# Holding k's scaling and the pooled q, k and v of a pair of heads behind the softmax of the pair one back

## The chip, the cores and the metric

One core of a Trainium2 chip runs the whole program. The metric is the device time of one execution in microseconds (us). The engines are TensorE (PE, with its weight loads as PEld), VectorE (DVE), ScalarE (ACT), GpSimd (POOL) and the DMA queue of SyncE (SPq).

## What is computed

q, k and v have 2 batches of 8 heads, 576 positions and 64 columns. Each head's attention is the sum of two: a local one, in which a position sees those fewer than 4 away, and a pooled one on the means of 4 neighbouring positions, whose result is repeated 4 times. The result x (1152 tokens of 512) goes through a gated layer and then through 8 experts that share the tokens:

```python
q_d = q.reshape(B, H, Sd, factor, D).mean(axis=3)   # k_d and v_d alike
out_up = np.repeat(sm_attn(q_d, k_d, v_d), factor, axis=2)
mask = np.abs(pos[:, None] - pos[None, :]) < factor
scores = np.where(mask, scale * np.matmul(q, k.transpose(0, 1, 3, 2)), -1000000000.0)
...
x = (silu(x @ w_gate) * (x @ w_val)) @ w_out
...
out += P[:, e:e + 1] * (np.maximum(x @ w1[e], 0.0) @ w2[e])
```

## The kernel before

**Attention.** Heads are worked in 8 pairs (pr 0 to 7; a head h is one of 0 to 15). For a pair, `pooled` scales k on ACT (L368) and makes the pooled k and q by sums of 4 on DVE (kd L369, qd L376), with a small scaling of kd on ACT (L370). `scores` of a head writes a mask and the products of five windows of 128 into PSUM (tiles s, L390 to L397) and the pooled products (L399). DVE takes the row minima (stm, L402 to L404), ACT seven exponentials per head (ex, L408 to L413) that also add up the rows, DVE adds and inverts the sums (rs, L416 and L417), and POOL multiplies ex by them (L419, L421). `turn` transposes ex on PE (t, L430 to L435) and ACT copies it out (at, L436 to L438). `combine` multiplies a pair's two heads by v and by the pooled v (o, L450 and L457); DVE adds both parts up as x (L466), and `split` cuts x into two f16 halves, xhl, the high one on ACT (L166) and the low one on DVE (L167). `pooled_v` makes the pooled v (vdz) by three additions on POOL (L381 to L383). `x1_scale` finds a scale for all of a batch's x by products of v on PE (vv, L341), whose maximum DVE reads (mxv, L344).

**Beside it** the weights of the gated layer are prepared. `conv_gv` turns one of 12 blocks of 64-bit numbers (rawg, 1 MB each) into f32: one operation on ACT (L198, or L195 from the sixth block on), four on DVE (cvg, L199 to L202), and a largest value on ACT (L217). `prep_gv` splits the block into two f16 halves (gv, L166 and L167). `gv_step(c, f)` is 24 or 48 products by block f for the tokens of chunk c, and a few operations on ACT and DVE behind them (act, L543 to L560). Chunk 0 holds the first 512 tokens, which pairs 0 to 3 complete; chunk 1 needs all pairs. So gv(0,0) to gv(0,3) can run on PE while batch 1 is still in attention, and gv(1,0) ends the dependence on it. The rest (output layer, routing, experts) follows, most of it products on PE.

**What sets the order.** `attention` is a generator that is advanced step by step; scores run four heads ahead of the transposes (AHEAD). A list scheduler gives each engine a fixed order of instructions, in which it works strictly one after the other: an instruction that waits holds back all behind it. A block under `gate(x)` puts its instructions of x's engine behind x in that order; it adds no semaphore. Buffers also bind: k and q have 3 slots, v4 has 4, the PSUM tiles s, t and o share 6 banks (two per tile), rawg and cvg have 2 buffers each.

Of the kernel before, what the change touches and what calls it, by code (L numbers as in the profile page):

```python
# [11 lines left out]
AF = mybir.ActivationFunctionType  # L12
ALU = mybir.AluOpType
AX = mybir.AxisListType
# [4 lines left out]
FAC, SD = 4, 144  # L19
# [5 lines left out]
HS = SD // 2  # L25
# [13 lines left out]
DO = NW * P  # L39
# [21 lines left out]
def tile_kernel(ctx, tc, qT, kT, vw, vd4, wgv, wo, wg2, w1, w2, out):  # L61
    nc = tc.nc
    V, A, G, T = nc.vector, nc.scalar, nc.gpsimd, nc.tensor
# [143 lines left out]
    def gate(after):  # L207
        return tc.issue_after(after.ins) if after else nullcontext()
# [148 lines left out]
    def attention():  # L357
# [2 lines left out]
            return [psa.tile([P, 512], F32, tag="att", bufs=6, name=f"{nm}_{i}") for i in range(2)]  # L360

        qd, kd, exs, ats = {}, {}, {}, {}

        def pooled(pr):
            q, k = qz[pr % NQ], ld[pr]
            qd[pr] = ap.tile([P, 2, SD], F32, tag="qd", name=f"qd{pr}")
            kd[pr] = ap.tile([P, SD], F32, tag="kd", name=f"kd{pr}")
            A.activation(k, k, AF.Copy, scale=-0.125)  # L368
            V.tensor_reduce(kd[pr], k.rearrange("p (s a) -> p s a", a=FAC), axis=AX.X, op=ALU.add)  # L369
            A.activation(kd[pr], kd[pr], AF.Copy, scale=1.0 / (FAC * FAC))  # L370
            if pr not in QDV:
                t = ap.tile([P, 2, 2 * SD], F32, tag="qt", bufs=1, name=f"qt{pr}")
                G.tensor_tensor(t, q[:, :, 0::2], q[:, :, 1::2], op=ALU.add)
                G.tensor_tensor(qd[pr], t[:, :, 0::2], t[:, :, 1::2], op=ALU.add)
            else:
                V.tensor_reduce(qd[pr], q.rearrange("p j (s a) -> p j s a", a=FAC), axis=AX.X, op=ALU.add)  # L376

        def pooled_v(pr):
            v4, vd = v4s[pr], vdz[pr % 2]
            vt = ap.tile([HS, 2, 2, P], F32, tag="vt", bufs=1, name=f"vt{pr}")  # L380
            G.tensor_tensor(vt[:, 0], v4[:, :, 0], v4[:, :, 1], op=ALU.add)  # L381
            G.tensor_tensor(vt[:, 1], v4[:, :, 2], v4[:, :, 3], op=ALU.add)
            G.tensor_tensor(vd, vt[:, 0], vt[:, 1], op=ALU.add)  # L383

        def scores(h):
            pr, j = h // 2, h % 2
            q, k = qz[pr % NQ], ld[pr]
            nm = f"{h}"
            ps = bank(f"s{nm}")
            T.matmul(ps[0], lhsT=identb, rhs=maskb.rearrange("p u w -> p (u w)"), start=True, stop=False)  # L390
            for w in range(NW - 1):
                ws = slice(WSTART[w], WSTART[w] + P)
                T.matmul(ps[0][:, w * P:(w + 1) * P], lhsT=q[:, j, ws], rhs=k[:, ws],
                         start=False, stop=w == NW - 2)
            T.matmul(ps[1][:, DW:DW + P], lhsT=identb, rhs=maskb[:, 0], start=True, stop=False)
            ws = slice(WSTART[4], WSTART[4] + P)
            T.matmul(ps[1][:, DW:DW + P], lhsT=q[:, j, ws], rhs=k[:, ws], start=False, stop=True)  # L397
            for t in range(2):
                T.matmul(ps[1][:HS, t * SD:(t + 1) * SD], lhsT=qd[pr][:, j, t * HS:(t + 1) * HS],  # L399
                         rhs=kd[pr], start=True, stop=True)  # L400
            mx, sm = stm[h % 2], sts[h % 2]
            V.tensor_reduce(mx[:, :4], ps[0].rearrange("p (u w) -> p u w", u=4), axis=AX.X, op=ALU.min)  # L402
            V.tensor_reduce(mx[:, 4:5], ps[1][:, DW:DW + P], axis=AX.X, op=ALU.min)
            V.tensor_reduce(mx[:HS, 5:7], ps[1][:HS, :DW].rearrange("p (u w) -> p u w", u=2),  # L404
                            axis=AX.X, op=ALU.min)
            ex = ap.tile([P, NW * P + DW], F32, tag="ex", bufs=6, name=f"ex{nm}")
            for w in range(4):
                A.activation(ex[:, w * P:(w + 1) * P], ps[0][:, w * P:(w + 1) * P], AF.Exp, scale=-1.0,  # L408
                             bias=mx[:, w:w + 1], accum_out=sm[:, w, 0:1])
            A.activation(ex[:, DO - P:DO], ps[1][:, DW:DW + P], AF.Exp, scale=-1.0,  # L410
                         bias=mx[:, 4:5], accum_out=sm[:, 4, 0:1])
            for t in range(2):
                A.activation(ex[:HS, DO + t * SD:DO + (t + 1) * SD], ps[1][:HS, t * SD:(t + 1) * SD], AF.Exp,  # L413
                             scale=-1.0, bias=mx[:HS, 5 + t:6 + t], accum_out=sm[:HS, 5 + t, 0:1])
            rs = ap.tile([P, 8], F32, tag="rs", name=f"rs{nm}")
            V.tensor_reduce(rs, sm, axis=AX.X, op=ALU.add)  # L416
            V.reciprocal(rs, rs)  # L417
            x = ex[:, :DO].rearrange("p (w k) -> p w k", w=NW)
            G.tensor_tensor(x, x, rs[:, :NW, None].to_broadcast([P, NW, P]), op=ALU.mult)  # L419
            x = ex[:HS, DO:].rearrange("p (t k) -> p t k", t=2)  # L420
            G.tensor_tensor(x, x, rs[:HS, 5:7, None].to_broadcast([HS, 2, SD]), op=ALU.mult)  # L421
            exs[h] = ex

        def turn(h):
# [430 lines left out]
```

## Time and profile before

| | us |
|---|---|
| median of 3 runs (lowest, highest) | 1033.76 (1032.47, 1036.16) |
| profiled execution, first to last instruction | 1030.5 |
| median less that span (what lies around it) | 3.3 |
| PE busy, share of the span | 1002.1, 97% |
| DVE busy | 757.6, 74% |
| ACT busy | 456.2, 44% |
| POOL busy | 77.7, 8% |

The page gives no time of its own for the profiled execution, so the span is set against the median of the runs. Busy shares are means over stages: attention takes the first tenth of the span, and there DVE, ACT and POOL work hardest; afterwards PE runs almost without a pause. Times of rows count from the span's start.

### The profile page before, as it was taken

To read this page: it belongs to the slowest core of one execution; us is meant where nothing else is said; L and a number is where in the kernel's file an instruction comes from. 1 tells how busy PE (TensorE), PEld (TensorE's weight loads), DVE (VectorE), ACT (ScalarE), POOL (GpSimd) and SP (SyncE) were. 2 spreads that over 40 slices of the span, in tenths; PEclk is the share of its full clock that TensorE was granted. 3 is DMA by queue.
4 is the path that set the end of the run, shared out by engine and by line. 5 is a ranking of instruction groups with operands and counts; after the bars stand their busy time and mean duration, and the time that the engine had idled before them with its cause. 6 is when DMAs were issued, how large, how long until landed. Compare 5 with 4: busy or idle time off the path is not lost.

```text
span 1030.5 us, 16425 instructions
## 1 busy us (share of the span) xinstructions
PE 1002.1 (97%) x6545; PEld 637.1 (62%) x6545; DVE 757.6 (74%) x1556; ACT 456.2 (44%) x957; POOL 77.7 (8%) x100
## 2 busy tenths in 40 slices
PE   5889999999999999999999999999999999999998
PEld 4776555665568657556565756656665575565644
DVE  5799688885765998697488759749766984974721
ACT  6899547675443745254145215323512521541300
POOL 5575000000000200000000000000000000000000
PEclk9999999999999999999999999999999999999999
DMA  9632224230020013103012112101301211020011
GB/s 222 194 102 73 111 89 164 109 137 1 1 83 1 17 66 123 42 5 118 1 42 83 41 41 79 45 3 40 123 1 42 82 42 41 1 83 1 1 41 52
DMA packets 13115, 65.54 MB, mean 64 GB/s; under 512 B 1712, under 2 KB 1968, under 8 KB 6640
## 3 DMA queue, kind: packets, MB, share of 16 engines
q1 hardware_dynamic: 13040, 64.51, 17.8%
q8 instruction: 51, 0.84, 0.3%
q14 instruction: 24, 0.20, 0.1%
HBM read 62.14 MB, written 2.36 MB: 63 GB/s over the span
## 4 chain that ended last, share of the span: by engine, by line
PE 82%; DVE 9%; DMA 4%; ACT 3%; issue 2%; SPq 0%; ACTq 0%; DVEq 0%
PE y L174 36%; PE p L174 31%; PE gv L174 9%; PE wo L174 4%; DMA vz<-in_vw 1%; DMA rawg<-in_wgv 1%; DMA rawo<-in_wo 1%; DMA k<-in_kT 1%; DVE cvg L201 1%; DVE w L167 1%; DVE xhl L167 1%; PE lgps L585 1%; DVE cvg L202 1%; ACT ex L408 0%; DMA qz<-in_qT 0%
## 5 line engine op out<-in xcount | busy, mean ns | idle before, releaser
L174 PE MATMUL y<-w,hhl 128*128 128x512 f16 (+1 forms) x1752 | 396.2, 376 | 0.0
L174 PE MATMUL p<-bop,w 128*128 128x320 f16 (+1 forms) x2688 | 354.4, 286 | 0.8 <-DVE u L727 0.5
L174 PEld LDWEIGHTS <-w 128*128 128x128 f16 x2688 | 263.0, 98 | 90.6 <-issue 1.3
L174 PEld LDWEIGHTS <-hhl 128*128 128x128 f16 x1752 | 171.5, 98 | 178.2
L755 ACT ACTIVATE hhl<-h 128x640 f16<-128x640 f32 (+1 forms) x128 | 83.2, 676 | 160.9 <-DVE h L727 160.9
L174 PE MATMUL gv<-xhl,gv 128*128 128x320 f16 (+1 forms) x864 | 142.3, 326 | 3.4 <-ACT act L556 1.4
L166 ACT ACTIVATE w<-r,s_w 128x256 f16<-128x256 f32 (+1 forms) x96 | 71.2, 783 | 117.3 <-PE y L174 86.3
L786 DVE SCALAR_TENSOR_TENSOR acc<-y,pe,acc 128x512 f32<-128x512 f32 (+1 forms) x64 | 47.3, 738 | 101.3 <-PE y L174 100.5
L174 PEld LDWEIGHTS <-gv 128*128 128x128 f16 x864 | 84.2, 98 | 59.5 <-issue 5.5
L756 DVE SCALAR_TENSOR_TENSOR hhl<-h,hhl 128x640 f16<-128x640 f32 (+1 forms) x128 | 94.3, 753 | 15.5 <-ACT hhl L755 14.2
L727 DVE SCALAR_TENSOR_TENSOR h<-p,u 128x256 f32<-128x256 f32 (+1 forms) x192 | 84.9, 452 | 19.3 <-PE p L174 13.5
L167 DVE SCALAR_TENSOR_TENSOR w<-r,s_w,w 128x256 f16<-128x256 f32 (+1 forms) x96 | 78.0, 832 | 16.7 <-ACT w L166 16.7
L174 PE MATMUL wo<-ahl,wo 128*128 128x320 f16 (+1 forms) x432 | 71.5, 326 | 0.0
L166 ACT ACTIVATE w<-cmb,s_w 128x512 f16<-128x512 f32 x64 | 43.0, 710 | 42.1 <-DVE cmb L271 39.9
L727 DVE SCALAR_TENSOR_TENSOR u<-p,u 128x320 f32<-128x320 f32 (+1 forms) x128 | 57.3, 448 | 4.1 <-PE p L174 3.2
L174 PEld LDWEIGHTS <-wo 128*128 128x128 f16 x432 | 42.3, 99 | 26.9
L153 POOL PARTITION_ALL_REDUCE g_w<-gm_w x16 | 6.3, 394 | 592.7 <-DVE gm_w L149 586.7
L744 ACT ACTIVATE s<-p 128x256 f32<-128x256 f32 (+1 forms) x64 | 25.4, 397 | 55.8 <-PE p L174 55.7
L143 DVE TENSOR_REDUCE mxw<-r 128x1 f32<-128x1024 f32 x32 | 37.4, 1213 | 12.8 <-DMA r<-in_w 12.8
L167 DVE SCALAR_TENSOR_TENSOR w<-cmb,s_w,w 128x512 f16<-128x512 f32 x64 | 46.0, 740 | 0.1
L291 ACT ACTIVATE j<-r 128x1024 f16<-128x1024 f32 x32 | 33.4, 1046 | 25.4 <-DMA r<-in_w 25.4
L167 DVE SCALAR_TENSOR_TENSOR ahl<-act,sc,ahl 128x512 f16<-128x512 f32 (+1 forms) x24 | 19.6, 818 | 17.1 <-ACT ahl L166 17.1
(199 smaller groups left out, 914.8 us busy)
## 6 DMA issues: line engine op xcount, KB each, us to landing
r<-in_w SPq DMA_DIRECT2D x32, 1024.0 KB, 4.8
rawg<-in_wgv SPq DMA_DIRECT2D x12, 1024.0 KB, 4.8
rawo<-in_wo SPq DMA_DIRECT2D x6, 1024.0 KB, 6.8
vz<-in_vw SPq DMA_DIRECT2D x8, 320.0 KB, 5.9
k<-in_kT SPq DMA_DIRECT2D x8, 288.0 KB, 3.5
qz<-in_qT SPq DMA_DIRECT2D x16, 144.0 KB, 5.0
v<-in_vd SPq DMA_DIRECT2D x8, 288.0 KB
out<-acc SPq DMA_DIRECT2D x8, 256.0 KB, 2.0
```

The source lines that it names most:

```text
L143: V.tensor_reduce(o, i, axis=axis, op=ALU.max, apply_absolute_value=True)
L166: return (A.activation(hi, src, AF.Copy, scale=s), V.scalar_tensor_tensor(lo, src, s, hi, op0=ALU.mult, op1=ALU.subtract))
L167: V.scalar_tensor_tensor(lo, src, s, hi, op0=ALU.mult, op1=ALU.subtract))
L174: T.matmul(ps, lhsT=wf(i, k), rhs=xf(j, k), start=n == 0, stop=n == 3 * nk - 1)
L201: V.scalar_tensor_tensor(o, hi, 0xC0000000, o, op0=ALU.bitwise_and, op1=ALU.bitwise_or)
L202: V.scalar_tensor_tensor(o, lo, 29, o, op0=ALU.logical_shift_right, op1=ALU.bitwise_or)
L291: A.activation(junk, t[:, 2 * j:2 * j + 2].rearrange("p a n -> p (a n)"), AF.Abs, accum_out=mx[:, 2 * i + j:2 * i + j + 1])
L727: V.scalar_tensor_tensor(o, ps, HSC, u, op0=ALU.mult, op1=ALU.add)
L744: A.activation(s1, p1, AF.Copy, scale=HSC)
L755: ra = A.activation(t[:, 0], h, AF.Relu)
L756: rv = V.scalar_tensor_tensor(t[:, 1], h, 0.0, t[:, 0], op0=ALU.max, op1=ALU.subtract)
L786: V.scalar_tensor_tensor(acc[t][:, ds], ps, p[:, t:t + 1], acc[t][:, ds], op0=ALU.mult, op1=ALU.add)
```

## The change

Three dictionaries keep, for each head, its last exponential on ACT (`exped`), its reciprocal on DVE (`summed`) and its last multiplication on POOL (`scaled`). From the third pair on, k's scaling is put behind the last exponential of the pair one back, and the pooled k and q behind its reciprocal. The pooled v of the second to eighth pair is put behind the last multiplication of the pair one back. No instruction is added or taken away.

```diff
--- before.py
+++ after.py
@@ -360,27 +360,32 @@
             return [psa.tile([P, 512], F32, tag="att", bufs=6, name=f"{nm}_{i}") for i in range(2)]
 
         qd, kd, exs, ats = {}, {}, {}, {}
+        exped, summed, scaled = {}, {}, {}
 
         def pooled(pr):
             q, k = qz[pr % NQ], ld[pr]
             qd[pr] = ap.tile([P, 2, SD], F32, tag="qd", name=f"qd{pr}")
             kd[pr] = ap.tile([P, SD], F32, tag="kd", name=f"kd{pr}")
-            A.activation(k, k, AF.Copy, scale=-0.125)
-            V.tensor_reduce(kd[pr], k.rearrange("p (s a) -> p s a", a=FAC), axis=AX.X, op=ALU.add)
+            with gate(exped.get(2 * pr - 1) if pr > 1 else None):
+                A.activation(k, k, AF.Copy, scale=-0.125)
+            with gate(summed.get(2 * pr - 1) if pr > 1 else None):
+                V.tensor_reduce(kd[pr], k.rearrange("p (s a) -> p s a", a=FAC), axis=AX.X, op=ALU.add)
             A.activation(kd[pr], kd[pr], AF.Copy, scale=1.0 / (FAC * FAC))
             if pr not in QDV:
                 t = ap.tile([P, 2, 2 * SD], F32, tag="qt", bufs=1, name=f"qt{pr}")
                 G.tensor_tensor(t, q[:, :, 0::2], q[:, :, 1::2], op=ALU.add)
                 G.tensor_tensor(qd[pr], t[:, :, 0::2], t[:, :, 1::2], op=ALU.add)
             else:
-                V.tensor_reduce(qd[pr], q.rearrange("p j (s a) -> p j s a", a=FAC), axis=AX.X, op=ALU.add)
+                with gate(summed.get(2 * pr - 1) if pr > 1 else None):
+                    V.tensor_reduce(qd[pr], q.rearrange("p j (s a) -> p j s a", a=FAC), axis=AX.X, op=ALU.add)
 
         def pooled_v(pr):
             v4, vd = v4s[pr], vdz[pr % 2]
             vt = ap.tile([HS, 2, 2, P], F32, tag="vt", bufs=1, name=f"vt{pr}")
-            G.tensor_tensor(vt[:, 0], v4[:, :, 0], v4[:, :, 1], op=ALU.add)
-            G.tensor_tensor(vt[:, 1], v4[:, :, 2], v4[:, :, 3], op=ALU.add)
-            G.tensor_tensor(vd, vt[:, 0], vt[:, 1], op=ALU.add)
+            with gate(scaled.get(2 * pr - 1)):
+                G.tensor_tensor(vt[:, 0], v4[:, :, 0], v4[:, :, 1], op=ALU.add)
+                G.tensor_tensor(vt[:, 1], v4[:, :, 2], v4[:, :, 3], op=ALU.add)
+                G.tensor_tensor(vd, vt[:, 0], vt[:, 1], op=ALU.add)
 
         def scores(h):
             pr, j = h // 2, h % 2
@@ -410,15 +415,16 @@
             A.activation(ex[:, DO - P:DO], ps[1][:, DW:DW + P], AF.Exp, scale=-1.0,
                          bias=mx[:, 4:5], accum_out=sm[:, 4, 0:1])
             for t in range(2):
-                A.activation(ex[:HS, DO + t * SD:DO + (t + 1) * SD], ps[1][:HS, t * SD:(t + 1) * SD], AF.Exp,
-                             scale=-1.0, bias=mx[:HS, 5 + t:6 + t], accum_out=sm[:HS, 5 + t, 0:1])
+                e = A.activation(ex[:HS, DO + t * SD:DO + (t + 1) * SD], ps[1][:HS, t * SD:(t + 1) * SD], AF.Exp,
+                                 scale=-1.0, bias=mx[:HS, 5 + t:6 + t], accum_out=sm[:HS, 5 + t, 0:1])
+            exped[h] = e
             rs = ap.tile([P, 8], F32, tag="rs", name=f"rs{nm}")
             V.tensor_reduce(rs, sm, axis=AX.X, op=ALU.add)
-            V.reciprocal(rs, rs)
+            summed[h] = V.reciprocal(rs, rs)
             x = ex[:, :DO].rearrange("p (w k) -> p w k", w=NW)
             G.tensor_tensor(x, x, rs[:, :NW, None].to_broadcast([P, NW, P]), op=ALU.mult)
             x = ex[:HS, DO:].rearrange("p (t k) -> p t k", t=2)
-            G.tensor_tensor(x, x, rs[:HS, 5:7, None].to_broadcast([HS, 2, SD]), op=ALU.mult)
+            scaled[h] = G.tensor_tensor(x, x, rs[:HS, 5:7, None].to_broadcast([HS, 2, SD]), op=ALU.mult)
             exs[h] = ex
 
         def turn(h):
```

What it does to the engines' orders is shown at three places. Numbers in names are those of heads (ex, s, at, t, stm), pairs (k, kd, qd, x, o) or weight blocks (rawg, cvg, gv); the last number of a name is the buffer's. Lines of the changed kernel stand five or six further down.

ACT at the start, from the exponentials of head 2 to the first transposed copy. Before:

```order
L370 ACTIVATE kd2_321<-kd2_321 128x144
L368 ACTIVATE k3_217<-k3_217 128x576
L408 ACTIVATE ex2_251,sts0_114<-s2_0_237,stm0_112 128x128 x4
L410 ACTIVATE ex2_251,sts0_114<-s2_1_238,stm0_112 128x128
L413 ACTIVATE ex2_251,sts0_114<-s2_1_238,stm0_112 72x144 x2
L368 ACTIVATE k4_291<-k4_291 128x576
L408 ACTIVATE ex3_278,sts1_115<-s3_0_264,stm1_113 128x128 x4
L410 ACTIVATE ex3_278,sts1_115<-s3_1_265,stm1_113 128x128
L413 ACTIVATE ex3_278,sts1_115<-s3_1_265,stm1_113 72x144 x2
L370 ACTIVATE kd3_506<-kd3_506 128x144
L198 ACTIVATE cvg0_312<-rawg0_310 128x1024
L436 COPY at0_297<-t0_0_295 128x512
```

With the change, from the exponentials of head 3 to those of head 4:

```order
L413 ACTIVATE ex3_278,sts1_115<-s3_0_264,stm1_113 128x128 x4
L415 ACTIVATE ex3_278,sts1_115<-s3_1_265,stm1_113 128x128
L418 ACTIVATE ex3_278,sts1_115<-s3_1_265,stm1_113 72x144 x2
L442 COPY at0_297<-t0_0_295 128x512
L443 COPY at0_297<-t0_1_296 128x128
L444 COPY at0_297<-t0_1_296 72x288
L370 ACTIVATE k2_146<-k2_146 128x576
L198 ACTIVATE cvg0_312<-rawg0_310 128x1024
L373 ACTIVATE kd2_321<-kd2_321 128x144
L217 ACTIVATE rawg0_310,mxg0_318<-cvg0_312 128x1024
L413 ACTIVATE ex4_340,sts0_114<-s4_0_326,stm0_112 128x128 x4
L442 COPY at1_355<-t1_0_353 128x512
```

k3, k4, kd2 and kd3 no longer stand among the exponentials of heads 2 and 3. The copies of head 0 moved ahead of the first weight block (cvg0), and k2, kd2 and the block's largest value (rawg0) now stand between them and head 4.

DVE where the scores of batch 1 (vv1) are read, before:

```order
L369 TENSOR_REDUCE kd7_1148<-k7_730 128x144
L376 TENSOR_REDUCE qd7_1147<-qz1_106 128x288
L167 SCALAR_TENSOR_TENSOR gv0_615<-cvg0_312,s_gv0_622,gv0_615 128x1024
L416 TENSOR_REDUCE rs10_823<-sts0_114 128x8
L344 TENSOR_REDUCE mxv1_932<-vv1_899 128x1
L417 RECIPROCAL rs10_823<-rs10_823 128x8
L346 TENSOR_TENSOR mxv1_932<-mxv1_932,mxv0_432 128x1
L416 TENSOR_REDUCE rs11_865<-sts1_115 128x8
L417 RECIPROCAL rs11_865<-rs11_865 128x8
```

and with the change:

```order
L202 SCALAR_TENSOR_TENSOR cvg2_632<-rawg2_630,cvg2_632 128x1024
L422 TENSOR_REDUCE rs10_823<-sts0_114 128x8
L158 TENSOR_REDUCE gr_gv1_767<-sm_gv1_766 1x1
L423 RECIPROCAL rs10_823<-rs10_823 128x8
L344 TENSOR_REDUCE mxv1_932<-vv1_899 128x1
L422 TENSOR_REDUCE rs11_865<-sts1_115 128x8
L346 TENSOR_TENSOR mxv1_932<-mxv1_932,mxv0_432 128x1
L423 RECIPROCAL rs11_865<-rs11_865 128x8
L380 TENSOR_REDUCE qd6_992<-qz0_105 128x288
L372 TENSOR_REDUCE kd6_993<-k6_580 128x144
```

The pooled q and k of pair 6 now stand behind the reading of vv1; those of pair 7 stood ahead of it.

DVE at the row minima of head 14, before:

```order
L416 TENSOR_REDUCE rs12_1020<-sts0_114 128x8
L158 TENSOR_REDUCE gr_gv1_767<-sm_gv1_766 1x1
L417 RECIPROCAL rs12_1020<-rs12_1020 128x8
L416 TENSOR_REDUCE rs13_1062<-sts1_115 128x8
L402 TENSOR_REDUCE stm0_112<-s14_0_1153 128x4
L417 RECIPROCAL rs13_1062<-rs13_1062 128x8
L136 TENSOR_SCALAR u_gv1_771<-sm_gv1_766 128x1
L466 TENSOR_TENSOR x14_1085<-o4_0_1067,avd4_1083 128x364
L466 TENSOR_TENSOR x14_1085<-o4_1_1068,avd4_1083 128x212
L137 TENSOR_SCALAR u_gv1_771<-u_gv1_771 128x1
L403 TENSOR_REDUCE stm0_112<-s14_1_1154 128x1
L404 TENSOR_REDUCE stm0_112<-s14_1_1154 72x2
```

and with the change:

```order
L372 TENSOR_REDUCE kd7_1148<-k7_730 128x144
L200 TENSOR_SCALAR cvg3_969<-cvg3_969 128x1024
L550 TENSOR_SCALAR act0_0_1099<-act0_0_1099,iv0_0_1096 128x512
L138 TENSOR_SCALAR s_gv2_959<-u_gv2_958 128x1
L139 TENSOR_SCALAR i_gv2_960<-u_gv2_958 128x1
L167 SCALAR_TENSOR_TENSOR xhl_134<-x14_1085,s_x11_944,xhl_134 128x576
L201 SCALAR_TENSOR_TENSOR cvg3_969<-rawg3_967,cvg3_969 128x1024
L551 TENSOR_TENSOR act0_0_1099<-act0_0_1099,gv0_0_00_1100 128x512
L528 TENSOR_SCALAR iv0_2_1421<-i_gv2_960,i_x10_444 128x1
L407 TENSOR_REDUCE stm0_112<-s14_0_1153 128x4
L167 SCALAR_TENSOR_TENSOR gv2_952<-cvg2_632,s_gv2_959,gv2_952 128x1024
L202 SCALAR_TENSOR_TENSOR cvg3_969<-rawg3_967,cvg3_969 128x1024
```

Operations on weight blocks 2 and 3 (gv2, cvg3), on the first gated product (act0_0) and the low half of x14 moved ahead of the minima of head 14; the pooled q and k of pair 7 came down to just before them.

## Rows read from the trace of the kernel before

**Rows 1.** Busy time of each engine in two stretches (us and instructions)

```profile
50.00:75.00 25.00, 21.72 (x224) 19.45 (x224) 23.95 (x55) 23.61 (x96) 18.20 (x19) 1.00 0.34 116
75.00:100.00 25.00, 23.81 (x222) 18.45 (x221) 24.00 (x59) 23.60 (x84) 15.84 (x15) 1.00 0.21 70
```

**Rows 2.** Timeline of the start: start, duration, engine, line, operation, count [idle before, releaser]

```profile
17.87 0.58 SPq L183 DMA_DIRECT2D rawg<-in_wgv  x1
...
19.13 1.35 DVE L376 TENSOR_REDUCE qd<-qz 128x288 f32<-128x1152 f32 x1 [2.18 <-DMA qz<-in_qT]
...
20.40 0.16 DVE L416 TENSOR_REDUCE rs<-sts 128x8 f32<-128x16 f32 x1
...
22.25 1.25 POOL L419 TENSOR_TENSOR ex<-ex,rs 128x640 f32<-128x640 f32 x1
...
23.56 1.12 PE L430 MATMUL t<-ident,ex 128*128 128x128 f32 x4 [8.01 <-POOL ex L419]
...
24.25 0.68 ACT L368 ACTIVATE k<-k 128x576 f32<-128x576 f32 x1 [2.35 <-DMA k<-in_kT]
...
27.48 1.17 ACT L198 ACTIVATE cvg<-rawg 128x1024 f32<-128x1024 f32 x1
```

**Rows 3.** DMA issues from 15 to 30 us: size, median us from issue to landing

```profile
rawg<-in_wgv SPq DMA_DIRECT2D x1, 1024.0 KB, 9.4
```

**Rows 4.** Timeline of ACT from the largest value of a block to head 10

```profile
57.37 1.06 ACT L217 ACTIVATE rawg<-cvg 128x1024 f16<-128x1024 f32 x1
...
58.42 0.35 ACT L408 ACTIVATE ex<-s,stm 128x128 f32<-128x128 f32 x1
...
59.79 0.69 ACT L368 ACTIVATE k<-k 128x576 f32<-128x576 f32 x1
...
60.54 0.38 ACT L410 ACTIVATE ex<-s,stm 128x128 f32<-128x128 f32 x1
...
61.59 0.59 ACT L436 COPY at<-t 128x512 f32<-128x512 f32 x1
...
62.51 0.36 ACT L370 ACTIVATE kd<-kd 128x144 f32<-128x144 f32 x1
62.73 0.75 ACT L166 ACTIVATE xhl<-x,s_x 128x512 f16<-128x512 f32 x1
63.34 0.39 ACT L408 ACTIVATE ex<-s,stm 128x128 f32<-128x128 f32 x1
```

**Rows 5.** Groups of DVE instructions, shapes apart, 0 to 106 us: busy us, mean ns

```profile
L402 DVE TENSOR_REDUCE stm<-s 128x4 f32<-128x512 f32 x16 | 10.8, 679 | 1.5 <-PE s L393 1.4
L376 DVE TENSOR_REDUCE qd<-qz 128x288 f32<-128x1152 f32 x8 | 10.7, 1343 | 3.1 <-DMA qz<-in_qT 3.1
L404 DVE TENSOR_REDUCE stm<-s 72x2 f32<-72x288 f32 x16 | 7.0, 439 | 0.0
...
L369 DVE TENSOR_REDUCE kd<-k 128x144 f32<-128x576 f32 x8 | 5.9, 735 | 0.0
...
L466 DVE TENSOR_TENSOR x<-o,avd 128x364 f32<-128x364 f32 x8 | 4.2, 519 | 0.5 <-ACT avd L460 0.5
L167 DVE SCALAR_TENSOR_TENSOR gv<-cvg,s_gv,gv 128x1024 f16<-128x1024 f32 x3 | 3.8, 1267 | 0.0
```

**Rows 6.** DVE's busy time on a weight block (tile cvg) in two stretches

```profile
48.10:57.40 9.30, 7.14 (x4) 1.00 0.43 153
100.60:106.00 5.40, 3.78 (x4) 1.00 0.55 194
```

**Rows 7.** PE's busy time on one pair's products by v (tile o)

```profile
75.60:77.40 1.80, 1.77 (x28) 1.00 0.00 0
```

**Rows 8.** Timeline of PE: products of v, and the last gated products before gv(1,0)

```profile
32.91 1.83 PE L341 MATMUL vv<-v 72*128 72x128 bf16 x29
...
106.05 12.89 PE L174 MATMUL gv<-xhl,gv 128*128 128x512 f16 x59 [1.24 <-DVE u_gv L136]
...
119.19 3.30 PE L174 MATMUL gv<-xhl,gv 128*128 128x512 f16 x22
```

## The prediction

> **What bounds the kernel now.** I read the page's busy shares first, then stretches of 25 us, then the timeline of each engine in attention. After 106 us PE hardly stops, so the time is decided by when PE can begin the unbroken run of gated products, and how much of that run it has already done by then. The two kernels do the same PE work; I therefore take the start of gv(1,0), 119.19 us in the profile [rows 8], as the mark that moves. Everything behind it I leave where it is relative to that mark.
>
> Between 50 and 100 us DVE is busy 23.95 and 24.00 of 25 us and ACT 23.61 and 23.60 [rows 1]: both are full, and time can be won there only by taking work away or by filling gaps before 50 us. Those gaps exist. In the start a pooled q waits 2.18 us for its DMA on DVE and a k waits 2.35 us on ACT, and behind them POOL multiplies head 0 only at 22.25 us, and PE, idle for 8.01 us, transposes it at 23.56 us [rows 2]. The change removes exactly these waits. But ACT reaches the first weight block at 27.48 us without waiting [rows 2], and that block was issued at 17.87 us and landed 9.4 us later, at 27.27 us [rows 2, 3].
>
> **The change part by part.** No instruction is added, so each part is a matter of order.
>
> *The start.* Without the wait of 2.18 us and the 1.27 us of pooled q (19.13 to 20.40) [rows 2] ahead of it, head 0's factor is ready near 16.9 us, POOL multiplies at about 17.1 us, and PE transposes at about 18.3 us: 5.2 us earlier. Heads 2 and 3 follow without k3 and k4, so ACT has done head 3, the copies of head 0 and k2 by about 22.4 us. Then it stands at cvg0, which cannot start before 27.27 us: a new wait of 4.9 us. Behind that operation stand kd2, without which head 4's pooled scores can't run, and the block's largest value, and only then head 4. So nothing of the 5.2 us gets past cvg0: it starts 0.2 us earlier than before, and pairs 3 and 4 have not been prepared.
>
> *From cvg0 to head 8.* A 128x1024 operation takes ACT 1.05 us from start to start, a head's exponentials 1.37 + 1.05 = 2.42, a head's copies 0.92, k with the small avd 0.75, kd 0.22, a high half of x 0.61 [rows 4]. cvg0 ends at 28.3; the four DVE operations of a block take 3.78 us of busy time when POOL is quiet [rows 6], 3.5 with the overlap of about 0.07 us that DVE shows between neighbours (1.35 us long, next start 1.27 later [rows 2]): 31.9. Then ACT works without a gap: rawg0 and rawg1 and cvg1 3 x 1.05, heads 4 to 7 9.7, four heads' copies 3.7, k3 and k4 with two avd 1.5, two high halves 1.2, two kd 0.4: 19.7 us, and an estimated 0.7 of waits for stm and o. Head 8 starts at 52.4.
>
> *To head 10.* ACT: head 8, head 9 but its last operation, copies of head 5, and gv0's high half: 6.5 us, 58.9. DVE has run dry and waits for that half, then does its low half (1.2), x12 and the factors of head 9 (1.0) [rows 5]: 61.1. Then kd5 0.66, qd5 1.27, three larger stm groups 1.8, three operations of cvg2 2.35, a low half of x about 0.7 (half of gv's): 6.8 us, 67.9.
>
> *The wait on vv1.* The last products for the scale of batch 1 now stand on PE behind o3, which needs head 10's PSUM back. Head 10 ends 1.05 us later, o3 takes 1.77 [rows 7], some 16 products of v at 0.063 (1.83 for 29 [rows 8]) 1.0: 71.7. DVE stands at mxv1 until then, and qd6 and kd6 behind it. They, x13 and the minima of head 12 take 3.8 us [rows 5]: 75.5.
>
> *Heads 12 to 15.* ACT: heads 12 and 13, one copy, gv1: 6.8, 82.3. DVE then has ahead of head 15's last minima: x14 0.73, qd7 1.27, kd7 0.66, the block cvg3 3.5, the low halves of tail, x14 and gv2 2.75, the three act0_0 operations 1.7, two heads' stm 2.3, eight small ones 0.8: 13.7, and 0.3 for head 13's factors: 96.3. Head 15's exponentials end 3.5 later, 99.8; the copies of heads 12 and 13, with twelve gated products between their transposes on PE, 4.0 later: 103.8. POOL's end to PE's start in the first transposes is 0.06 us (22.25 + 1.25 to 23.56) [rows 2]; ten such handovers make 0.6: 104.4.
>
> *The tail.* Less is left for PE than before, since gv(0,0) and half of gv(0,1) are done: 60 products at 12.89 / 59 = 0.218 [rows 8] 13.1, o7 and two thirds of o6 3.0, the transposes of head 15 and small ones 1.2: 17.3. gv(1,0) starts at 121.7.
>
> *Unknown: DVE beside POOL.* The same four operations of a block that took 3.78 us alone took 7.14 with POOL at work [rows 6], 3.4 us more. The new order has multiplications of heads 8, 9, 12 and 13 beside parts of cvg2 and cvg3. Bounds are 0 and 3.4 for each block; of the four operations only one or two fall beside POOL, so I take 1.1 each at most, 121.7 to 123.9, and the middle, 122.8, for the forecast. The Trainium skill (GPSIMD Engine Reference, Key points) says that POOL shares its SBUF interfaces with VectorE and contends with DVE instructions in a two-port mode or with two SBUF inputs. By that rule taken in full, with 3.4 us for each of the two blocks, the sum would be 128.5 at the mark; taken not at all, 121.7. The block at 48.10 us agrees with it.
>
> **The sum.** 122.8 - 119.2 = 3.6 us. The profiled span of 1030.5 us lies 3.3 us under the median of 1033.8; I leave that as it is: 1033.8 + 3.6 = **1037.4 us**. What this measurement can tell from no change is about 0.3%, 3.1 us.
>
> **The rivals.**
>
> *Faster: the early start carries through.* The transposes come 5.2 us earlier, and block 1's conversion no longer meets POOL's work (up to 3.4 us). If ACT's wait before cvg0 costs nothing because DVE was the later of the two from head 4 on, the mark moves by the 5.2 us: 1028.6. For it: ACT, DVE and PE all stand behind the DMA in the start [rows 2], and the two engines that are full later get rid of these gaps. Against it: the landing at 27.27 us [rows 2, 3]. It decides from head 8: there it would have to start near 47 us, not 52.4. Chance 0.24.
>
> *Same: PE pays back what attention loses.* The attention ends later, but PE does more gated products inside it. Copies of head 13 done at 119.2 - 17.3 = 101.9 would give exactly the old mark; my sum, 104.4 to 106.6, is 2.5 to 4.7 us off, so three of the estimated small waits wrong by a microsecond would do: 1033.8. The Trainium skill (Perfetto Trace Analysis, Identifying the Most-Contended Engine) says to work on the engine with the highest occupancy; by that, with PE at 97%, an order on ACT, DVE and POOL changes nothing, which is this case too. The trace agrees with it behind 106 us and not before, where PE waits for ACT and POOL [rows 2]. Chance 0.22 for a time within 1 us or so.
>
> *Slower by much: POOL beside both blocks.* With the full 3.4 us for cvg2 and for cvg3 the mark is at 121.7 + 6.8 = 128.5; DVE's two dry spells ahead of gv0 and of vv1 take up an estimated 1.5 us: 127.0, 7.8 us late, 1041.6. Against it: only one block of the two shown paid that much [rows 6]. Chance 0.10.
>
> **How the numbers follow.** My forecast, an attention that ends 1 to 6 us later, has 0.44, its own range 1034.8 to 1039.9; 0.30 of it lies over 3.1 us and 0.14 under. So slower 0.30 + 0.10 = 0.40, same 0.14 + 0.22 = 0.36, faster 0.24. The range that leaves out some 0.2 cuts part of the faster case and the end of the slow one: 1029.5 to 1042.
>
> **What would show it.** Right: POOL's first multiplication near 17 and PE's first transposes near 18.3 us; ACT waiting 4 to 5 us for the DMA of rawg before cvg; head 4 at about 33 and head 8 at about 52.4 us; DVE waiting a microsecond or more for vv before mxv; minima of head 15 at 96 to 98 us; gv(1,0) at 121.5 to 124 us. Wrong: cvg0 starting well before 27 us, or head 8 before 50; DVE idle little between 55 and 75; the mark at or before 119; or PE stalls behind the mark that differ by over a microsecond, which I have put at no change.

## The result and the profile after

The changed kernel took 1040.75 us (median of 4 runs, 1038.41 to 1041.99) against 1033.12 for the kernel before beside it (4 runs): ratio 1.0068, 95% interval 1.0045 to 1.0091. That is 7.0 us slower by the ratio. The forecast was 1037.4 in a range of 1029.5 to 1042. The profiled execution spans 1040.1 us, 9.6 us more than the one before; its time, 1041.99 us, is the highest of the four, so the two profiles lie further apart than the medians.

Busy time by stretches (length, then us and instructions of PE, PE's weight loads, DVE, ACT and POOL, granted clock, DMA share, GB/s); the last two rows answer to [rows 1], and the first row stands against the second, which is of the kernel before:

```profile
25.00:50.00 25.00, 17.27 (x114) 15.14 (x112) 12.72 (x30) 13.44 (x51) 8.15 (x11) 0.70 0.48 140
25.00:50.00 25.00, 21.45 (x207) 18.58 (x207) 18.41 (x42) 21.19 (x92) 12.95 (x16) 0.95 0.62 198
50.00:75.00 25.00, 21.41 (x197) 18.44 (x196) 21.92 (x49) 22.28 (x92) 14.54 (x14) 0.93 0.56 176
75.00:100.00 25.00, 22.67 (x201) 17.55 (x199) 23.00 (x62) 20.63 (x76) 14.47 (x14) 1.00 0.21 70
```

DVE and ACT, which were full from 50 to 100 us, now have gaps of 2 to 4.4 us per stretch, and from 25 to 50 us both stand about half the time (12.72 and 13.44 us busy, against 18.41 and 21.19). The timeline of the start shows where (start, duration, engine, line, operation, idle before and what ended it), against [rows 2]:

```profile
18.42 0.41 SPq L183 DMA_DIRECT2D rawg<-in_wgv  x1
23.08 0.32 SPq L319 DMA_DIRECT2D v<-in_vd  x1
...
16.43 1.25 POOL L425 TENSOR_TENSOR ex<-ex,rs 128x640 f32<-128x640 f32 x1
...
17.74 0.66 PE L436 MATMUL t<-ident,ex 128*128 128x128 f32 x4 [2.57 <-POOL ex L425]
...
21.86 0.81 ACT L370 ACTIVATE k<-k 128x576 f32<-128x576 f32 x1
31.61 1.12 ACT L198 ACTIVATE cvg<-rawg 128x1024 f32<-128x1024 f32 x1 [8.95 <-DMA rawg<-in_wgv]
...
32.77 0.69 DVE L199 TENSOR_SCALAR cvg<-cvg 128x1024 f32<-128x1024 f32 x1 [9.22 <-ACT cvg L198]
...
36.80 1.06 ACT L217 ACTIVATE rawg<-cvg 128x1024 f16<-128x1024 f32 x1 [3.86 <-DVE cvg L202]
37.85 0.35 ACT L413 ACTIVATE ex<-s,stm 128x128 f32<-128x128 f32 x1
```

The early start is there (POOL 5.8 us, PE 5.8 us earlier) and ACT loses it at the block: it stands 8.95 us at cvg, then 3.86 us for DVE's four operations on the block, and head 4 begins at 37.85. The block itself came later than before [rows 3], and v of the fifth pair was issued during its flight:

```profile
rawg<-in_wgv SPq DMA_DIRECT2D x1, 1024.0 KB, 13.2
```

Late in attention a second place shows: head 14's exponentials begin 9.2 us behind the end of head 13's, against 2.1 before. DVE works without a pause from 89.65 to 97.89 us ahead of head 14's minima. The pooled q and k of pair 7, gated there, are 1.9 us of it; operations on blocks 2 and 3, on the first gated product and on halves of x, which the new order has put ahead of these minima, are most of the rest (ACT and DVE rows by time):

```profile
91.46 0.75 ACT L370 ACTIVATE k<-k 128x576 f32<-128x576 f32 x1
...
94.30 0.32 ACT L373 ACTIVATE kd<-kd 128x144 f32<-128x144 f32 x1 [0.40 <-DVE kd L372]
...
98.60 0.37 ACT L413 ACTIVATE ex<-s,stm 128x128 f32<-128x128 f32 x1 [2.09 <-DVE stm L407]
...
90.66 1.34 DVE L380 TENSOR_REDUCE qd<-qz 128x288 f32<-128x1152 f32 x1
...
93.53 0.73 DVE L372 TENSOR_REDUCE kd<-k 128x144 f32<-128x576 f32 x1
...
97.89 0.68 DVE L407 TENSOR_REDUCE stm<-s 128x4 f32<-128x512 f32 x1
```

The mark, PE's first product of 320 columns (gv(1,0)), moved from about 119.5 us to about 129.3. The last row of [rows 8], from 119.19, opens with a product of 512 columns; and in the second from 129 us two products of 512 columns come first, from 128.8 on, at some 0.22 us each.

```profile
L174 PE MATMUL gv<-xhl,gv x8: 299/299/379, 128.8 to 129.9; 128*128 128x320 f16 x6, 128*128 128x512 f16 x2
```

That is 9.8 us, and the span grew by 9.6: nothing much happens behind the mark in these two executions. It is so in nearly all that follow: span less mark lies between 909.3 and 911.9 us in twelve of the fourteen profiled executions (913.4 in e2, 915.2 in e3). A second way to add it up is PE's lost time: in rows of 1 us, the idle part plus, of the busy part, the share that the granted clock is under 1. Over the first 180 us it is 24.8 us before (22.8 idle, 2.0 lost at 1.2 GHz) and 33.9 after (22.0 and 11.9): 9.1 of the 9.6 us, and 9.0 of it lies between 25 and 50 us (4.8 before, 13.8 after). So in these two executions PE does not stand longer than before; it works longer at 1.2 GHz. PE stood almost all of 27 to 33 us, and behind that it was granted 0.53 and 0.57 of the clock:

```profile
27.00:33.00 6.00, 0.09 (x2) 0.01 (x1) 0.23 (x1) 1.33 (x2) 0.40 (x1) 0.75 0.47 123
33.00:37.00 4.00, 4.00 (x19) 3.98 (x20) 3.90 (x5) 0.20 (x1) 0.00 (x0) 0.53 0.01 2
40.00:48.00 8.00, 8.00 (x54) 6.54 (x52) 4.46 (x17) 6.93 (x29) 5.15 (x7) 0.57 0.59 202
```

### The profile page after: what moved, and what is told of

Same layout as the page of the kernel before. It is cut to its first block, busy times and chain, and to the rows that moved or that the text cites. A ratio compares the mean times of both kernels' runs of the same rounds, so it can differ in the third digit from the quotient of the medians.

```text
span 1040.1 us, 16428 instructions
## 1 busy us (share of the span) xinstructions
PE 1011.6 (97%) x6545; PEld 643.6 (62%) x6545; DVE 753.2 (72%) x1556; ACT 457.5 (44%) x957; POOL 75.3 (7%) x100
## 4 chain that ended last, share of the span: by engine, by line
PE 79%; DVE 10%; ACT 6%; DMA 3%; issue 2%; ACTq 0%; DVEq 0%
PE y L174 36%; PE p L174 31%; PE gv L174 5%; PE wo L174 4%; DMA rawg<-in_wgv 2%; ACT ex L413 1%; DMA qz<-in_qT 1%; DMA rawo<-in_wo 1%; DVE cvg L201 1%; DVE w L167 1%; DVE act L563 1%; DVE cvo L201 1%; PE o L463 1%; DVE cvo L202 1%; PE lgps L591 1%
## 5 line engine op out<-in xcount | busy, mean ns | idle before, releaser
L733 DVE SCALAR_TENSOR_TENSOR h<-p,u 128x256 f32<-128x256 f32 (+1 forms) x192 | 84.6, 451 | 18.3 <-PE p L174 12.4
L291 ACT ACTIVATE j<-r 128x1024 f16<-128x1024 f32 x32 | 33.4, 1045 | 25.1 <-DMA r<-in_w 25.1
L733 DVE SCALAR_TENSOR_TENSOR u<-p,s 128x256 f32<-128x256 f32 (+1 forms) x64 | 28.7, 449 | 4.7 <-PE p L174 4.0
```

Source lines behind the costliest of these rows:

```text
L291: A.activation(junk, t[:, 2 * j:2 * j + 2].rearrange("p a n -> p (a n)"), AF.Abs, accum_out=mx[:, 2 * i + j:2 * i + j + 1])
L733: V.scalar_tensor_tensor(o, ps, HSC, u, op0=ALU.mult, op1=ALU.add)
```

## The experiments

The runs were made in four groups: e1 to e4, e5 to e8, e9 to e11, e12. All times are medians; ratios are to the kernel before, run beside on the same chip. The change was run only with its own four runs of before, so where its ratio is set against another, differences of up to 0.3% lie within the two intervals. The columns of heads give where POOL's multiplication of heads 4, 8 and 15 starts in the profiled execution, mark is the start of gv(1,0) in it; lost is PE's lost time in its first 180 us, added up as above; clock is the granted clock's mean over all runs of that kernel.

| kernel | us | ratio, 95% interval | head 4 | head 8 | head 15 | mark | lost | clock |
|---|---|---|---|---|---|---|---|---|
| before | 1033 | 1 | 34.9 | 61.7 | 91.3 | 119.5 | 24.8 | 0.992 |
| the change | 1040.75 | 1.0068 (1.0045 to 1.0091) | 42.8 | 64.8 | 107.9 | 129.3 | 33.9 | 0.989 |
| e1 v of pair 5 loaded later | 1041.27 | 1.0081 (1.0060 to 1.0102) | 39.9 | 62.4 | 105.6 | 126.9 | 30.7 | 0.986 |
| e2 block 0 behind head 5 | 1037.20 | 1.0034 (1.0012 to 1.0056) | 29.6 | 55.3 | 97.1 | 120.9 | 23.9 | 0.990 |
| e3 gates of pairs 2 to 4 only | 1039.62 | 1.0073 (1.0047 to 1.0099) | 42.4 | 66.9 | 106.7 | 128.8 | 31.9 | 0.988 |
| e4 gates of pairs 5 to 8 only | 1046.18 | 1.0119 (1.0097 to 1.0141) | 35.0 | 63.2 | 106.3 | 131.2 | 34.0 | 0.987 |
| e5 as e3, block 0 behind head 5 | 1035.80 | 1.0030 (1.0014 to 1.0046) | 34.1 | 60.8 | 87.2 | 123.5 | 27.8 | 0.991 |
| e6 no gates, block 0 behind head 5 | 1040.01 | 1.0059 (1.0040 to 1.0079) | 32.3 | 63.7 | 96.7 | 126.2 | 32.3 | 0.988 |
| e7 gates of pair 8 only | 1034.66 | 1.0009 (0.9995 to 1.0023) | 35.2 | 61.7 | 96.3 | 120.4 | 25.1 | 0.993 |
| e8 no DVE gates | 1036.29 | 1.0027 (1.0014 to 1.0040) | 39.1 | 61.6 | 100.9 | 123.7 | 28.7 | 0.990 |
| e9 all gates, block 0 loaded earlier | 1038.91 | 1.0050 (1.0031 to 1.0069) | 34.7 | 57.3 | 100.9 | 122.3 | 25.9 | 0.988 |
| e10 as e3, block 0 loaded earlier | 1037.39 | 1.0055 (1.0033 to 1.0077) | 35.4 | 60.7 | 91.7 | 120.6 | 24.6 | 0.991 |
| e11 no gates, block 0 loaded earlier | 1036.21 | 1.0029 (1.0014 to 1.0044) | 39.0 | 65.8 | 95.4 | 123.6 | 27.8 | 0.989 |
| e12 DVE gates only | 1035.21 | 1.0033 (1.0018 to 1.0048) | 40.4 | 63.6 | 104.0 | 121.8 | 25.0 | 0.991 |

The table splits the loss of the change. Against before, head 4 comes 7.9 us later, head 8 only 3.1, head 15 16.6, and the mark 9.8. From head 8 to head 15 it takes 41.9 to 43.6 us in the five kernels in which all gates of the later pairs (5 to 8) stand (the change, e1, e2, e4, e9), against 29.6 before and 26.4 to 33.0 in e5, e6, e10 and e11, which have none of them. With some of them it takes 34.6 to 40.4 (e7, e8, e12). e3, also without them, does not fit (39.9).

**e1: the load that flew beside the block.**

```diff
-                for i in range(2, NPAIR + 1):
+                for i in range(2, NPAIR):
                     load_v4(i)
...
             start(h + AHEAD)
+            if h == 1:
+                load_v4(NPAIR)
```

> Edit: of the changed kernel, only the load of v of the fifth pair is issued behind the loads of the sixth pair, as it was before the change; ACT, DVE, POOL and PE keep the changed kernel's order. In the changed kernel that load (288 KB) was issued at 23.08 us, while the first weight block rawg (issued 18.42) was on its way, and rawg landed at 31.59, 13.2 us after its issue against 9.4 before. Theory A (the start: ACT stands at cvg for a block that lands late because another transfer runs beside it): 288 KB at the 0.2 MB per us of that stretch is 1.4 us, so rawg lands near 30.2, cvg starts there, and the time falls from 1040.8 to about 1039.4. Rival B (the gates of the later pairs cost the time, the start is made good again): rawg earlier or not, the time stays at 1040.8. Rival C (the longer flight is not from the load that was moved): rawg lands at 31 or later again.

The same two views of this run, DMA issues and ACT's timeline:

```profile
rawg<-in_wgv SPq DMA_DIRECT2D x1, 1024.0 KB, 11.4
```

```profile
29.22 1.12 ACT L198 ACTIVATE cvg<-rawg 128x1024 f32<-128x1024 f32 x1 [6.73 <-DMA rawg<-in_wgv]
```

The block landed 2.4 us earlier, heads 4, 8 and 15 came 2.9, 2.4 and 2.3 us earlier, the mark 2.3, and the profiled span fell by 2.4 to 1037.7. So in the profiled executions a microsecond at cvg is a microsecond at the end of attention, as Theory A has it. The median did not follow (by itself it would speak for Rival B); these runs had the lowest clock of all kernels here, more on that below. The block landed at 29.2 us, earlier than Theory A (30.2) and Rival C (31 or later) have it. Nor is the moved load shown to be what delays the block. Its flight took 9.4 us (before, e7), 9.5 (e4), 9.9 (e8), 10.2 (e12), 10.3 (e6) and 11.4 (e1) without that load issued during it, and 10.1 (e2), 11.7 (e5), 12.2 (e3) and 13.2 (the change) with it: the two sets overlap, though most flights with it are longer. The Trainium skill (DMA: Bandwidth & Descriptors, Queues, rings and completion order) says that each DMA engine takes the descriptors of one queue in order, but that a later one may finish its write first. By that order alone a load issued 4.7 us behind would not start ahead of the block's; no run here decides whether it can hold up the block's landing.

**e2, e5, e6: the block's first operation behind head 5.** The loads stay where they are; conv_load is the load taken out of conv_gv.

```diff
         if n == AHEAD:
-            conv_gv(0)
+            conv_load(0)
+        if n == 8:
+            conv_gv(0, exped[5])
```

> Edit: of the changed kernel, the loads stay where they are, but ACT's first operation on weight block 0 and its largest value are issued behind head 5's exponentials, so that nothing of heads 4 and 5 stands behind the wait for that block. Theory A: ACT's idle 8.95 us before cvg and 3.86 us before the block's largest value, and DVE's 9.2 us, go; head 4 starts near 26 us instead of 37.85, head 8 near 50 to 52 instead of 59.25, and the start of gv(1,0) moves from 129 back to 119 to 122: 1031 to 1034. Rival B (the later pairs' gates cost the time): the start gains, the steady part loses it again, and the time stays within 2 us of 1040.8.

> Edit: the gates of the second to fourth pair only, and block 0's first ACT operation behind head 5's exponentials. What the runs so far say: the gates of the first pairs bring the first transposes 5 us forward and lose it at cvg; the gates of the later pairs lose time by themselves (1046.2 with them alone), since each pair's k, q and pooled scores become a chain between two pairs' softmax (in the run with cvg0 behind head 5 ACT waited 3.1 us for head 8's minima and head 14 came 13.5 us behind head 13). Theory A2 (both losses are separate): without either, the early start carries through: ACT never over 2 us idle between 25 and 60 us, head 15's multiplication on POOL at 88 us or before against 91.3 in the kernel before, 1026 to 1031. Rival B2 (the gates of the first pairs lose time also without the wait for the block): 1034 or more.

> Edit: no gate at all (the order rules of the kernel before), and block 0's first ACT operation behind head 5's exponentials. The fourth corner of the table {all gates, first pairs' gates, none} by {cvg0 as it was, behind head 5}. Theory A2: before the change ACT never waited over 1.5 us for the block, so moving it gains nothing: 1032 to 1036. Rival (the block's place is what gains in the other runs, and the gates do nothing): under 1030.

In e2 head 4 is 13.2 us earlier than in the change and head 8 9.5, better than the forecast for the start; then a pair's boundary costs, as this row of ACT at head 8 shows:

```profile
49.72 0.37 ACT L420 ACTIVATE ex<-s,stm 128x128 f32<-128x128 f32 x1 [3.12 <-DVE stm L414]
```

The mark, 120.9, is Theory A's (119 to 122); the time, 1037.2, lies between the two theories. In e5 head 15's multiplication comes at 87.2 us, 4.1 ahead of before, as Theory A2 has it. But ACT waits 2.60 us for k and 3.17 for block 1, the mark is 4.0 us later than before, and the time, 1035.80, is Rival B2's. An earlier end of attention is thus not enough by itself: PE lost 27.8 us in e5, against 24.8. The three together with before, e3 and the change make a table: with the block where it was, gates cost 0.7% (1.0073 with those of the first pairs, 1.0068 with all); with the block behind head 5, the kernel without gates is the slowest (1.0059) and gates win 0.3% (1.0030 and 1.0034). For the gates of the first pairs the sign hangs on the block; the gain of all gates (1.0059 to 1.0034) is within the noise. Both parts of e6's expectation fell: moving the block alone costs 6 us, I had expected nothing or a gain.

**e3 and e4: the gates of the first pairs, and of the later ones, alone.**

```diff
-            with gate(exped.get(2 * pr - 1) if pr > 1 else None):
+            with gate(exped.get(2 * pr - 1) if 1 < pr < 4 else None):
```

and the same condition at the other gates; in e4 it is `pr > 3`.

> Edit: the gates of ACT, DVE and POOL are kept for the second to fourth pair only; the fifth to eighth are ordered as before the change. Theory A: the loss is made in the start, so this one is slow too: rawg awaited by ACT for over 7 us, 1038 to 1042. Rival B: with the later gates gone the time returns to 1033, within 2 us.

> Edit: the reverse of the run before: the gates are kept for the fifth to eighth pair only. Theory A: no wait of over 3 us for rawg before cvg, and the time is that of the kernel before, 1031 to 1036. Rival B: the gates of the later pairs carry the loss, 1038 to 1042.

Theory A's time held for e3 (1039.62; there ACT waited 3.48 us for k and then 4.66 us for the block, not 7 for the block alone) and failed for e4, the slowest of all at 1046.18. So both theories were half of it: the gates of the later pairs cost by themselves. Why they cost more alone than all gates together is not shown. In e4 ACT's rows show the chain at the last boundary, and the stretches behind it what PE pays:

```profile
89.22 0.76 ACT L370 ACTIVATE k<-k 128x576 f32<-128x576 f32 x1
92.53 0.40 ACT L373 ACTIVATE kd<-kd 128x144 f32<-128x144 f32 x1
97.08 0.37 ACT L413 ACTIVATE ex<-s,stm 128x128 f32<-128x128 f32 x1 [3.12 <-DVE stm L407]
```

```profile
96.00:100.00 4.00, 2.15 (x25) 1.62 (x25) 4.00 (x7) 2.92 (x12) 0.00 (x0) 1.00 0.00 0
100.00:111.00 11.00, 9.93 (x53) 7.01 (x50) 7.78 (x17) 9.40 (x36) 4.44 (x5) 0.53 0.36 122
```

PE stood 1.85 us there, and the products of v, the transposes and the first gated products that follow up to 111 us ran mostly at 1.2 GHz (0.53 granted).

**e7: one boundary.** The kernel before with the gates of the eighth pair only (`if pr == 7` at each gate).

> Edit: the kernel before with the gates of the eighth pair alone: its k scaling behind head 13's exponentials, its pooled k and q behind head 13's factors, its pooled v behind head 13's multiplication. Theory A2 (the chain at a pair's boundary costs): head 14's multiplication on POOL comes 10 to 14 us behind head 13's instead of 4.8, the end of attention moves 5 to 10 us; PE has gated products to do meanwhile, so the time moves by about half of it: 1036 to 1039. Rival (PE's products cover it all): 1033, within 2 us.

Theory A2 missed and the rival held: head 14's multiplication did come 8.5 us behind head 13's (4.8 before) and head 15's 5 us later, but the time is 1.0009 of before. One late boundary is covered by gated products (PE lost 25.1 us, against 24.8); the loss of e4 comes from several, or from earlier ones, which no run here separates.

**e8 and e12: without DVE's gates, and with them alone.** In e8 DVE's two gates go; in e12 those of ACT and POOL go instead, in the same way.

```diff
-            with gate(summed.get(2 * pr - 1) if pr > 1 else None):
+            with gate(None):
                 V.tensor_reduce(kd[pr], k.rearrange("p (s a) -> p s a", a=FAC), axis=AX.X, op=ALU.add)
...
-                with gate(summed.get(2 * pr - 1) if pr > 1 else None):
+                with gate(None):
                     V.tensor_reduce(qd[pr], q.rearrange("p j (s a) -> p j s a", a=FAC), axis=AX.X, op=ALU.add)
```

> Edit: the changed kernel without the gates of DVE (pooled k and pooled q); those of ACT and POOL stay. In its order v of the fifth pair is loaded behind the sixth pair's loads again, as before the change. Theory A2: rawg lands 9.4 to 11.5 us behind its issue, ACT still stands at cvg for 3 us or more, the later pairs keep most of their chain through ACT's k scaling: 1037 to 1041. Rival D (DVE's gates alone make the loss): 1034 or less.

> Edit: the kernel before with DVE's gates alone (pooled k and q of the third to eighth pair behind the factors of the pair one back); k's scaling on ACT and pooled v on POOL are free. The complement of the run without DVE's gates (1036.3). DVE's gates are what brings the first transposes forward, what puts the fifth pair's v behind the block's load, and what places 1.9 us of DVE work between two pairs' softmax. Theory D (DVE's gates carry the loss): the first multiplication on POOL at 16.5 us, rawg 12 us or more in flight, ACT waiting 3 us or more for it, 1038 to 1042. Rival E (it takes ACT's gate as well: k's scaling, pooled k and its copy in one chain behind the exponentials): 1033 to 1036.

Theory D fell and Rival E held; e8 lies between its two theories (ACT stood 2.69 us at cvg, where 3 or more were expected). Each half costs about 0.3%, and the two together come to nearly the 0.7% of the whole. Neither half brings the first multiplication forward (21.98 us in e8, 22.40 in e12): with ACT's gates alone DVE waits 5.00 us for q's load, with DVE's alone ACT waits 2.74 us for k's. It takes both to start early, and only with both does ACT stand 9 us at the block. So most of what each half costs by itself is not that wait.

**e9, e10, e11: the wait's cause taken away.** The block is loaded ahead of the third and fourth pair's v and the fifth pair's q and k.

```diff
                 pooled_v(0)
-                for i in range(2, NPAIR + 1):
+                conv_load(0)
+                for i in range(2, NPAIR):
                     load_v4(i)
```

> Edit: the changed kernel, all gates kept; the load of weight block 0 is issued right behind the fourth pair's loads, ahead of the third and fourth pair's v (576 KB) and the fifth pair's q and k (576 KB), and the fifth pair's v goes behind the sixth pair's loads. ACT's order stays that of the changed kernel but for cvg standing ahead of k2. It takes the wait's cause away, not the wait. Theory A: 1152 KB at the 0.2 MB per us of that stretch are 5 us and more, so rawg is there by about 23 to 25 us instead of 31.6, ACT waits 0 to 3 us for it; head 4's multiplication on POOL comes near 35 us instead of 42.8, head 8's near 57 instead of 64.8; the time falls by 5 to 7 us to 1034 to 1036. What stays over 1033 is the later pairs' chain. Rival B (the later pairs' gates alone make the loss): within 2 us of 1040.8.

> Edit: the same move of the block's load with the gates of the second to fourth pair only. Theory A: neither the wait for the block nor the later chain is left: 1027 to 1032, under the kernel before. Rival (the order of the list scheduler behind the start decides, whatever the start gains): 1033 or more.

> Edit: the same move of the block's load in the kernel before, without any gate. It shows what the earlier load is worth where ACT hardly waited for the block (1.5 us idle for DMA rawg in the first stretch of the kernel before). Theory A: 1031 to 1034, no gain to speak of. Rival (the earlier load is a gain of its own, gates or not): under 1030, and e9's gain is not from the wait that the gates made.

e9's rows of ACT, DVE and POOL:

```profile
21.49 1.15 ACT L198 ACTIVATE cvg<-rawg 128x1024 f32<-128x1024 f32 x1 [0.30 <-DMA rawg<-in_wgv]
...
29.50 1.06 ACT L224 ACTIVATE rawg<-cvg 128x1024 f16<-128x1024 f32 x1 [4.19 <-DVE cvg L202]
...
22.67 1.63 DVE L199 TENSOR_SCALAR cvg<-cvg 128x1024 f32<-128x1024 f32 x1 [0.68 <-ACT cvg L198]
...
24.88 1.18 DVE L200 TENSOR_SCALAR cvg<-cvg 128x1024 uint32<-128x1024 uint32 x1
26.09 1.64 DVE L201 SCALAR_TENSOR_TENSOR cvg<-rawg,cvg 128x1024 uint32<-128x1024 uint32 x1
...
27.86 1.55 DVE L202 SCALAR_TENSOR_TENSOR cvg<-rawg,cvg 128x1024 uint32<-128x1024 uint32 x1
...
23.69 1.13 POOL L434 TENSOR_TENSOR ex<-ex,rs 72x288 f32<-72x288 f32 x1
...
25.59 1.06 POOL L393 TENSOR_TENSOR vt<-v 72x256 f32<-72x256 f32 x1
26.62 1.71 POOL L394 TENSOR_TENSOR vt<-v 72x256 f32<-72x256 f32 x1
...
34.69 1.25 POOL L432 TENSOR_TENSOR ex<-ex,rs 128x640 f32<-128x640 f32 x1 [6.37 <-DVE rs L430]
...
57.28 1.26 POOL L432 TENSOR_TENSOR ex<-ex,rs 128x640 f32<-128x640 f32 x1 [1.18 <-DVE rs L430]
```

The wait of 8.95 us is 0.30, head 4 comes at 34.69 (expected near 35) and head 8 at 57.28 (near 57), head 15 still 7.0 us earlier, the mark too, and the profiled span is 1032.4. For the mechanism at this place that is Theory A. The median fell by less than expected, to 1038.91 where 1034 to 1036 stood, which is just inside the rival's bound; its runs go from 1034.46, the profiled one, to 1042.39. By the ratios (1.0068 and 1.0050) that gain is not clear of noise. In e10 the rival held (1037.39, though its profiled execution, the lowest of nine, took 1032.9), and in e11 both theories missed: 1036.21 where no change or a gain was expected. So in e11 moving that load costs 0.3% by itself, as moving the block's first operation costs 0.6% (e6), and neither of these two kernels has a gate. No version was faster than the kernel before.

## Why the prediction was right, and where its sizes were off

The side and the range held, and in the profiled execution the mechanism too: the early start is lost at the first weight block, and the later pairs then end attention later. The chain was 6.5 us short at the mark (129.3 against 122.8), and the time came out only 3.4 us over the forecast; that it came so near is in part luck, since the two profiles lie further apart than the medians. That these two places carry the loss of the medians is not shown: e10 has neither, and its median is still 0.55% over before.

- *The start* was right: POOL 16.43 (17.1 forecast), PE 17.74 (18.3), ACT at cvg from 22.66 (22.4).
- *"It cannot start before 27.27 us"* was taken for the time itself. This is the step that failed: the block landed at 31.59, 4.3 us later, so the wait was 8.95 and not 4.9 us. In e1 (2.4 us at cvg, 2.3 at head 15) and e9 (8.65 and 7.0) most of what is won there reaches the end of attention.
- *From cvg0 to head 8* was 24.1 us by the sum and took 26.6 (32.63 to 59.25). With the late landing that makes the 6.9 us that head 8 is late against 52.4. Behind it the chain held: head 15's minima ended at 103.3, 7.0 late against 96.3.
- *The wait on vv1*, 3.8 us in the sum (67.9 to 71.7), was not there: DVE comes to the row below with no idle time before it, busy since 65.91. From the pooled k of pair 5 to this row the sum had 10.6 us with that wait in it, and 9.4 us of work were measured (68.10 to 77.50). That the chain is right behind it is luck in part.

```profile
77.50 0.23 DVE L344 TENSOR_REDUCE mxv<-vv 128x1 f32<-128x128 f32 x1
```

- *DVE beside POOL*, 1.1 us for each of two blocks (cvg2 and cvg3): nearly nothing, 0.2 us. The rows of the changed kernel (ns min, median, max), against [rows 6], are at their quiet durations but for the first operation on cvg2 (879) and the last on cvg1 (1627):

```profile
L199 DVE TENSOR_SCALAR cvg<-cvg x5: 672/685/879, 32.8 to 111.5; 128x1024 f32<-128x1024 f32 x5
L200 DVE TENSOR_SCALAR cvg<-cvg x4: 677/679/694, 33.5 to 94.2; 128x1024 uint32<-128x1024 uint32 x4
L201 DVE SCALAR_TENSOR_TENSOR cvg<-rawg,cvg x4: 1207/1214/1226, 34.2 to 96.0; 128x1024 uint32<-128x1024 uint32 x4
L202 DVE SCALAR_TENSOR_TENSOR cvg<-rawg,cvg x4: 1207/1218/1627, 35.5 to 99.7; 128x1024 uint32<-128x1024 uint32 x4
```

  The rival built on it had the right time (1041.6) for the wrong reason. The effect itself is seen in e9: where POOL works beside the first block, the four operations take 1.63, 1.18, 1.64 and 1.55 us. The Trainium skill (GPSIMD Engine Reference, Key points) says that POOL shares its SBUF interfaces with VectorE; e9's rows are in line with it.
- *PE's clock* has no term in the sum. In PE's account above the whole difference of the profiled pair stands there (2.0 and 11.9 us lost at 1.2 GHz), behind the stand that the wait for the block makes. How much of it the later chain on ACT and DVE would have cost anyway is not separated.
- *"The profiled span lies under the median; I leave that as it is"* hid a term. In each of the 84 runs of before beside the experiments the time is 1.8 to 2.0 us over the span, so some 1.4 of the 3.3 us are that the profiled execution was quicker than the median. It had a mean clock of 0.997; the runs of before here have 0.992, those of the changed kernel 0.989. The clock's term (span times one less the mean clock) is 8.1 us on the mean of these 84 runs and 11.4 us in the 4 runs of the change; the rest of the span is 1023.2 and 1027.1. Within a kernel a microsecond of that term goes with 0.64 us of span (199 runs), so of the 7.3 us between the mean spans an estimated 2 us go with the clock and 5 are left for the waits. Against the change e9 took 2.7 us from the rest (1024.4) and added 1.0 to the clock's term, e1 took 2.5 (1024.6) and added 3.7. The profiled times of e1, e9 and e10 are also the lowest of 6, 8 and 9, and that of the change the highest of 4. Both are part of why repaired starts gain less in the median than in their profiles.
- *Faster and same* were well argued against. PE did more gated products inside attention, as the second rival said: 48 of the 96 of chunk 0 were done by the end of attention's last copy (117.0 us), against 24 before (100.3 us). Of the 16.6 us that head 15 is late the mark kept 9.8; these 24 products more, at 0.22 us, are an estimated 5 us of the difference.

Open: why the block's flight scatters between 9.4 and 13.2 us, and why e10, with neither the wait nor the later gates, is not under the kernel before. An untested rival is that any other order costs some of this, whatever the gates do: e6 and e11 lose 0.6 and 0.3% without a gate. The split of the 5 us between the first block and the later pairs is known only roughly (2.7 from e9, with a standard error of about 1.2, and the remainder).

## What to carry to other kernels

An operation that another order brings forward is worth its time only up to the next thing that can't move: follow each engine to the first instruction that waits for a DMA, and look at the order there first. A landing time read from one execution is an estimate with an error of its own (here up to 4 us), and belongs in the range as such. Work gated behind the softmax of the pair one back turns slack into a chain at each boundary; one boundary was covered here, several were not. A single profiled execution shows where time goes, but two of them can lie further apart, or nearer, than the medians.

## What the runs showed that was not expected

The same stall of PE can end at either clock. These stretches are of e2 and of the kernel before, at the same place of the program:

```profile
297.00:299.00 2.00, 0.49 (x5) 0.39 (x4) 2.00 (x4) 2.00 (x4) 0.00 (x0) 1.00 0.26 107
...
300.00:308.00 8.00, 8.00 (x39) 5.66 (x37) 0.97 (x2) 0.00 (x0) 0.00 (x0) 0.57 0.00 0
```

```profile
296.00:298.00 2.00, 0.57 (x5) 0.20 (x2) 2.00 (x4) 2.00 (x5) 0.00 (x0) 1.00 0.41 172
...
299.00:307.00 8.00, 8.00 (x64) 6.16 (x64) 1.43 (x3) 0.00 (x0) 0.00 (x0) 1.00 0.00 0
```

PE stood 1.51 us in e2 and 1.50 in the kernel before (1.43 of it inside the stretch shown). Behind it PE was granted 0.57 of the clock in e2, most of 8 us at 1.2 GHz and 39 products instead of 64, and 1.00 in the kernel before. Such falls come in some executions of a kernel and not in others: over the 12 runs of e2 the span goes from 1030.1 at a mean clock of 0.995 to 1040.8 at 0.985. In a kernel where PE is busy 97% of the time, a stall of 1.5 us can thus cost a further 3.4 us (8 us at 0.57), and differences under 0.3% between two kernels want many runs of each.
